# A 64-byte filler tile at the right end of SBUF, in a two-mixture kernel on one core

## The chip, the cores and the metric

The kernel runs on one core of one Trainium2 chip. The metric is the device time of one execution, in microseconds (us); less is better. Each core has a tensor engine (TensorE; PE in the profile, its weight loads PEld), a vector engine (DVE), a scalar engine (ACT), GpSimd (POOL) and a sync engine (SP) that issues the DMA transfers. All operands of these engines stand in SBUF (128 partitions) or, for results of TensorE, in PSUM.

## What is computed

A recurrent attention, a first mixture (three matrix products with a gating multiply) and a second mixture of 8 experts, whose weights are normalised by eight rounds over rows and columns. The second mixture takes most of the time:

```python
def _moe2_ref(x, w_gate, w1, w2):            # x: 3072 x 384
    logits = x @ w_gate
    P = np.exp(logits - logits.max())
    for _ in range(8):
        P /= P.sum(1, keepdims=True) + 1e-09
        P /= P.sum(0, keepdims=True) + 1e-09
        P *= N / E
    for e in range(E):                       # 8 experts
        h = np.maximum(x @ w1[e], 0.0)       # w1[e]: 384 x 1024
        ye = h @ w2[e]                       # w2[e]: 1024 x 384
        out += P[:, e:e + 1] * ye
```

## The kernel before

**The three parts.** Attention, the first mixture and the conversion of its float64 weights run first, interleaved, up to about 442 us. The second mixture follows as 64 phases (line 1141: `for n in range(N + 1)`); the first of them still runs beside the last products of the first mixture (`moe_x2`, its PSUM tile is `po`).

**A phase.** Phase n belongs to weight step k = n // 4 (one quarter of an expert) and to one batch, sb = n % 4. In it stand 15 products of a fast matrix-multiplication scheme (line 543, `ORDER`), each with 2 column halves j and 3 float32 pieces (high by high, high by low, low by high): 15 x 2 x 3 = 90 matmuls into PSUM tiles `zp` (`z_prod`, line 869). Their moving operand is a slice of `xc` with 256 columns, their stationary operand a slice of `w1c` with 128 columns. Between the products stand units of the output product of the phase before (`y_fill`, line 1039, called by `y_units`): 24 units with 3 matmuls each, 72 into PSUM tiles `yp`, with a moving operand `w2h` or `w2l` of 384 columns and a stationary operand `hh` or `hl`. So a phase of the middle holds 162 matmuls. Every one loads its own weights (LDWEIGHTS), in the order in which the program is written: the schedule is by hand (line 104) and no planner moves anything.

**Which buffer a phase uses.** `w1c` has three sets by i % 3 and `w2h`, `w2l` have four by i % 4, where i = 2k + j is the weight number (lines 640 and 659). Set 2 of `w1c` and sets 2 and 3 of `w2h`, `w2l` lie in the pool `m2` on the left side of SBUF; the other sets and all of `xc` lie in the pools `wp` and `m1` on the right side, which is filled from the upper end downwards. `hh` and `hl` are always in `m2`. So k % 3 decides where the weights of the `zp` matmuls stand (0: both halves on the right; 1: half j = 0 on the left; 2: half j = 1 on the left), and k % 2 decides where the moving operand of the `yp` matmuls stands (even: right, odd: left; the first phase of a k still uses those of the k before).

**The addresses.** A matmul operand begins at its tile's address plus a multiple of 512 bytes, so its remainder modulo 128 is that of the tile. In bytes within a partition, as the program places them:

```
tile                       pool, side     address before   mod 128   after    mod 128
xc0, xc1                   wp, right      149472, 161760     96      149408 ..  32
xc2, xc3                   m1, right       90080, 104416     96       90016 ..  32
w1c, sets 0 and 1          wp, right      145376 ...         96      145312 ..  32
w1c, set 2                 m2, left        71456 ...         32      the same   32
w2h, w2l, sets 0 and 1     m1, right      126944 ...         96      126880 ..  32
w2h, w2l, sets 2 and 3     m2, left        55072 ...         32      the same   32
hh, hl                     m2, left        22304 ...         32      the same   32
gh, gl, w34h, w34l (po)    moe, left       44896 ...         96      the same   96
```

Counted over the program before, 3960 of the 5760 `zp` matmuls have weights with remainder 96 and 1800 with 32, all with a moving operand at 96; of the 4608 `yp` matmuls, all with weights at 32, half have a moving operand at 96 and half at 32.

Of the kernel before, what the change touches and what calls it, by code (L numbers as in the profile page):

```python
# [11 lines left out]
F32 = mybir.dt.float32  # L12
# [49 lines left out]
def tile_rwkv_moe_sinkhorn_moe(  # L62
# [21 lines left out]
    P = 128  # L84
# [51 lines left out]
    for c in range(2):  # L136
        nc.scalar.activation(eye[64 * c:64 * c + 64, :], ident[64 * c:64 * c + 64, 64 * c:64 * c + 64], AF.Copy)
        nc.gpsimd.affine_select(out=mask[64 * c:64 * c + 64, :], in_=mask[64 * c:64 * c + 64, :],
                                compare_op=ALU.is_gt, fill=0.0, base=0, pattern=[[1, DP]],
                                channel_multiplier=-1)  # L140

    st_moe = ExitStack()
    moe = st_moe.enter_context(tc.tile_pool(name="moe", bufs=1))
# [1095 lines left out]
```

## Time and profile before

| | |
|---|---|
| three runs | 1945.58, 1946.57 and 1946.62 us, median 1946.57 |
| profiled execution, span from first to last instruction | 1946.4 us |
| PE busy | 1919.9 us, 99% of the span |
| DVE, ACT, POOL busy | 1381.8, 686.2, 647.2 us |
| DMA engines, mean busy share | 51.4% for the kernel's own transfers |
| granted TensorE clock | 1.00 (2.4 GHz) in every stretch |

The profile gives no total of its own for the profiled execution; its span is taken as its time. A row of the timeline shows when a run of like instructions starts and how many there are. Matmuls are pipelined: the duration that a row gives for one is longer than the distance from its start to the next start, and that distance is what a matmul costs where PE never idles. A row of the windows shows the busy time of each engine in a stretch, and the number of instructions with any part in it.

### The profile page before, as it was taken

What the parts mean: (1) busy time and instruction counts of PE and PEld (TensorE: products, weight loads), DVE (VectorE), ACT (ScalarE), POOL (GpSimd) and SP (SyncE); (2) the same over time, 40 slices, a digit from 0 to 9 for tenths busy, and PEclk for the clock granted to TensorE, in tenths of its full rate; (3) what the DMA queues carried; (4) which work ended last, traced back from release to release, by engine and by line L of the source; (5) the groups of instructions that cost most, each with busy time, mean ns of one, the idle gap of its engine ahead of it and who ended that gap; (6) DMA issues with size and microseconds to landing.
All of it is one profiled execution on the core that took longest, in us unless ns stands there. A gap on an engine that the chain in (4) does not pass through costs nothing.

```text
span 1946.4 us, 38115 instructions
## 1 busy us (share of the span) xinstructions
PE 1919.9 (99%) x15499; PEld 1872.1 (96%) x15499; DVE 1381.8 (71%) x2409; ACT 686.2 (35%) x1322; POOL 647.2 (33%) x867
## 2 busy tenths in 40 slices
PE   6999999999999999999999999999999999999999
PEld 3799999999999999999999999999999999999999
DVE  7865777765887876666767676666676767667666
ACT  6733333344333333233333233333333333333322
POOL 6856666635332312222222222221313231312200
PEclk9999999999999999999999999999999999999999
DMA  9632444347655555454545555555454555555453
GB/s 371 228 95 81 138 132 137 104 151 247 224 177 202 184 190 187 174 213 172 202 177 193 186 193 181 187 185 195 172 202 176 199 188 186 188 179 189 167 202 118
DMA packets 90494, 353.76 MB, mean 182 GB/s; under 512 B 10384, under 2 KB 34256, under 8 KB 64592
## 3 DMA queue, kind: packets, MB, share of 16 engines
q1 hardware_dynamic: 90320, 351.34, 51.4%
q8 instruction: 122, 2.00, 0.4%
q14 instruction: 52, 0.43, 0.1%
HBM read 329.67 MB, written 20.45 MB: 180 GB/s over the span
## 4 chain that ended last, share of the span: by engine, by line
PE 96%; DVE 2%; DMA 1%; ACT 1%; issue 0%; SPq 0%; DVEq 0%; ACTq 0%
PE yp L114 41%; PE zp L114 35%; PE po L114 5%; PE pa L114 5%; PE pb L114 4%; PE w34ps L114 2%; PE yt L114 1%; PE sc L114 1%; PE trn L114 1%; PE up L114 1%; DMA raw<-in_moe_w_out_dram 0%; PE pl L114 0%; DMA raw<-in_moe_w_dram 0%; DVE cvp L229 0%; DMA xraw<-xraw 0%
## 5 line engine op out<-in xcount | busy, mean ns | idle before, releaser
L114 PE MATMUL zp<-xc,w1c 128*128 128x256 f32 x5760 | 815.4, 281 | 1.0 <-DVE ct L894 0.5
L114 PEld LDWEIGHTS zp<-xc,w1c 128*128 128x128 f32 x5760 | 783.6, 189 | 3.8 <-DVE ct L897 1.4
L114 PE MATMUL yp<-w2h,hh 128*128 128x384 f32 x1536 | 516.9, 337 | 0.0
L114 PE MATMUL yp<-w2h,hl 128*128 128x384 f32 x1536 | 516.3, 336 | 0.5 <-DVE hl L891 0.5
L114 PE MATMUL yp<-w2l,hh 128*128 128x384 f32 x1536 | 513.9, 335 | 0.0
L886 ACT ACTIVATE hh<-ct 128x512 fp32r<-128x512 f32 x384 | 237.1, 632 | 538.1 <-DVE ct L894 269.8
L894 DVE TENSOR_TENSOR ct<-ct,zp 128x512 f32<-128x512 f32 x576 | 381.0, 683 | 53.2 <-PE zp L114 47.5
L616 POOL TENSOR_TENSOR w1c<-w1s,w1c 128x512 fp32r<-128x512 f32 (+1 forms) x120 | 127.7, 1064 | 796.4 <-PE yp L114 487.9
L901 ACT ACTIVATE ct<-zp 128x512 f32<-128x512 f32 x256 | 153.3, 599 | 455.9 <-PE zp L114 455.9
L114 PEld LDWEIGHTS yp<-w2h,hh 128*128 128x128 f32 x1536 | 290.9, 189 | 0.2 <-issue 0.2
L114 PEld LDWEIGHTS yp<-w2h,hl 128*128 128x128 f32 x1536 | 288.1, 188 | 1.0 <-DVE hl L891 0.9
L114 PEld LDWEIGHTS yp<-w2l,hh 128*128 128x128 f32 x1536 | 288.3, 188 | 0.0
L1066 DVE SCALAR_TENSOR_TENSOR acc<-yp,Pm,acc 128x384 f32<-128x384 f32 x336 | 205.5, 612 | 109.4 <-PE yp L114 109.2
L891 DVE SCALAR_TENSOR_TENSOR hl<-ct,hh 128x512 fp32r<-128x512 f32 x384 | 273.8, 726 | 0.0
L897 DVE TENSOR_TENSOR ct<-ct,zp 128x512 f32<-128x512 f32 x128 | 88.0, 688 | 168.4 <-PE zp L114 168.4
L897 DVE TENSOR_TENSOR ct<-zp,ct 128x512 f32<-128x512 f32 x128 | 88.3, 690 | 78.2 <-PE zp L114 69.6
L616 POOL TENSOR_TENSOR w1c<-w1raw,w1c 128x128 fp32r<-128x128 f32 (+1 forms) x90 | 55.0, 612 | 205.6 <-ACT w1c L612 205.6
L608 POOL TENSOR_TENSOR w1s<-w1raw 128x128 f32<-128x128 f32 x240 | 121.0, 525 | 0.2
L483 POOL TENSOR_TENSOR gl<-gs,gh 128x384 fp32r<-128x384 f32 x64 | 74.2, 1160 | 109.3 <-ACT gh L479 106.6
L114 PE MATMUL pa<-xhl,w1h 128*128 128x384 f32 x384 | 101.7, 345 | 1.2 <-ACT w34s L255 1.2
L114 PE MATMUL pb<-xhl,w2h 128*128 128x384 f32 x384 | 98.1, 336 | 0.4 <-DVE cv L230 0.4
L474 DVE TENSOR_TENSOR gs<-pb,asb 128x384 f32<-128x384 f32 x64 | 35.4, 553 | 71.5 <-PE pb L114 49.3
(130 smaller groups left out, 1906.2 us busy)
## 6 DMA issues: line engine op xcount, KB each, us to landing
xc<-xd SPq DMA_DIRECT2D x192, 1024.0 KB, 4.8
xc<-xd SPq DMA_DIRECT2D x64, 768.0 KB, 4.3
xd<-x2s SPq DMA_DIRECT2D x53, 256.0 KB, 2.8
w1raw<-in_e_w_dram SPq DMA_DIRECT2D x32, 384.0 KB, 3.1
w2raw<-in_e_w_dram SPq DMA_DIRECT2D x32, 384.0 KB, 3.1
raw<-in_moe_w_dram SPq DMA_DIRECT2D x8, 1024.0 KB, 8.9
nat_w<-in_w_dram SPq DMA_DIRECT2D x24, 264.5 KB, 3.3
nat_k<-in_kt_dram SPq DMA_DIRECT2D x24, 256.0 KB, 4.0
```

Of the source, the lines that this page charges most:

```text
L114: nc.tensor.matmul(o, lhsT, rhs, start=start, stop=stop, **kw)
L474: nc.vector.tensor_tensor(t, m_t.pop(("pb", blk, f)), m_t.pop(("asb", blk, f)), op=ALU.mult)
L483: nc.gpsimd.tensor_tensor(gl[:, f, :], m_t.pop(("gs", blk, f)), gh[:, f, :].bitcast(F32), op=ALU.subtract)
L608: eng.tensor_tensor(tmp_[:, many.index(r), :], at_(a), at_(b), op=ALU.add if sg == 1 else ALU.subtract)
L616: eng.tensor_tensor(lo[:, d0:d1, :], sv, hi[:, d0:d1, :].bitcast(F32), op=ALU.subtract)
L886: nc.scalar.activation(hh, src, AF.Relu)
L891: nc.vector.scalar_tensor_tensor(hl, src, 0.0, hh.bitcast(F32), op0=ALU.max, op1=ALU.subtract)
L894: nc.vector.tensor_tensor(o, a, b_, op=ALU.add)
L897: nc.vector.tensor_tensor(o, a, b_, op=ALU.subtract)
L901: nc.scalar.activation(t, src, AF.Copy)
L1066: nc.vector.scalar_tensor_tensor(dst, yp, so["Pm"][:, tt, e:e + 1], dst, op0=ALU.mult, op1=ALU.add)
```

## The change

The change adds a pool on the right side of SBUF, opened ahead of all other pools of that side, with one tile of 16 float32 (64 bytes in each partition). Nothing reads or writes the tile. Every later tile on the right side lies 64 bytes lower. No instruction is added, removed or moved, and every wait stays: the instructions of the two programs agree one by one but for addresses, on every engine.

```diff
@@ -138,6 +138,9 @@
         nc.gpsimd.affine_select(out=mask[64 * c:64 * c + 64, :], in_=mask[64 * c:64 * c + 64, :],
                                 compare_op=ALU.is_gt, fill=0.0, base=0, pattern=[[1, DP]],
                                 channel_multiplier=-1)
+
+    edge = ctx.enter_context(tc.tile_pool(name="edge", bufs=1, side="right"))
+    edge.tile([P, 16], F32, name="edge")
 
     st_moe = ExitStack()
     moe = st_moe.enter_context(tc.tile_pool(name="moe", bufs=1))
```

## Rows read from the trace of the kernel before

**Rows 1.** The page: span, busy time by engine, chain that ended last.
```profile
span 1946.4 us, 38115 instructions
...
PE 1919.9 (99%) x15499; PEld 1872.1 (96%) x15499; DVE 1381.8 (71%) x2409; ACT 686.2 (35%) x1322; POOL 647.2 (33%) x867
...
PE yp L114 41%; PE zp L114 35%; PE po L114 5%; PE pa L114 5%; PE pb L114 4%; PE w34ps L114 2%; PE yt L114 1%; PE sc L114 1%; PE trn L114 1%; PE up L114 1%; DMA raw<-in_moe_w_out_dram 0%; PE pl L114 0%; DMA raw<-in_moe_w_dram 0%; DVE cvp L229 0%; DMA xraw<-xraw 0%
```

**Rows 2.** Windows, four stretches; the second holds phases 4 to 62.
```profile
core 0: us, PE busy (x) PEld busy (x) DVE busy (x) ACT busy (x) POOL busy (x), PEclk, DMA share, GB/s
442.02:540.07 98.05, 96.47 (x677) 94.53 (x677) 70.11 (x132) 37.06 (x78) 45.99 (x64) 1.00 0.69 243
540.07:1907.07 1367.00, 1367.00 (x9569) 1365.27 (x9569) 969.80 (x1567) 445.10 (x821) 328.81 (x537) 1.00 0.53 188
0.00:442.02 442.02, 420.64 (x5021) 376.76 (x5022) 320.54 (x677) 197.38 (x415) 272.38 (x266) 1.00 0.47 158
1907.07:1946.40 39.33, 35.83 (x235) 35.49 (x234) 21.38 (x35) 6.64 (x11) 0.00 (x0) 1.00 0.25 86
```

**Rows 3.** Waits of PE: who, for whom, total us, times, longest.
```profile
PE sc L114 <- POOL Rt L312: 14.0, 1, 14.0
...
PE yp L114 <- DVE hl L891: 0.5, 1, 0.5
PE zp L114 <- DVE ct L894: 0.5, 1, 0.5
PE zp L114 <- DVE ct L897: 0.5, 2, 0.2
```

**Rows 4.** Windows on PE, one whole phase each: 39, 27, 31, 43, 47, 35.
```profile
core 0: us, PE busy (x), PEclk, DMA share, GB/s
1351.40:1374.59 23.19, 23.19 (x163) 1.00 0.48 170
1073.87:1097.18 23.32, 23.32 (x163) 1.00 0.48 170
1166.48:1189.50 23.02, 23.02 (x163) 1.00 0.50 172
1444.14:1467.41 23.27, 23.27 (x163) 1.00 0.49 170
1536.63:1559.73 23.09, 23.09 (x163) 1.00 0.47 171
1258.69:1281.73 23.04, 23.04 (x163) 1.00 0.48 172
```

**Rows 5.** Timeline of PE at the start of phase 39.
```profile
1351.40 0.87 PE L114 MATMUL zp<-xc,w1c 128*128 128x256 f32 x6
1352.11 0.34 PE L114 MATMUL yp<-w2h,hh 128*128 128x384 f32 x1
```

**Rows 6.** Timeline of PE at the start of phase 40.
```profile
1374.59 0.86 PE L114 MATMUL zp<-xc,w1c 128*128 128x256 f32 x6
1375.28 0.34 PE L114 MATMUL yp<-w2h,hh 128*128 128x384 f32 x1
```

**Rows 7.** Timeline of PE in phase 0, where `zp` alternates with `po`.
```profile
446.26 0.88 PE L114 MATMUL zp<-xc,w1c 128*128 128x256 f32 x6
...
456.79 0.88 PE L114 MATMUL zp<-xc,w1c 128*128 128x256 f32 x6
457.51 0.34 PE L114 MATMUL po<-gh,w34l 128*128 128x384 f32 x1
...
458.03 0.33 PE L114 MATMUL po<-gh,w34l 128*128 128x384 f32 x1
...
458.90 0.88 PE L114 MATMUL zp<-xc,w1c 128*128 128x256 f32 x6
459.61 0.34 PE L114 MATMUL po<-gl,w34h 128*128 128x384 f32 x1
```

## The prediction

> **What bounds the kernel now.** I read the page first: PE is busy for 1919.9 of 1946.4 us, and the chain that ended last is the row of PE's own matmuls, `yp` 41% and `zp` 35% [rows 1]. Then the windows by part: from 540.07 to 1907.07 us, phases 4 to 62, PE is busy all of 1367.00 us, while DVE is busy for 969.80, ACT for 445.10 and POOL for 328.81 of it [rows 2]. Then PE's waits: all that `zp` and `yp` wait for other engines are 1.5 us, and the one long wait, 14.0 us, belongs to attention [rows 3]. The granted clock is 1.00, 2.4 GHz, in each stretch [rows 2]. So in 59 of 64 phases the time is the number of matmuls times the distance from start to start, and nothing else. The change alters no instruction and no wait; it can act only by making that distance longer or shorter, or not at all.
>
> Next I cut the span at the starts of phases. A phase holds the same 162 matmuls every time, and yet not all take as long [rows 4]. Phases differ in where their operands stand, which k % 3 and k % 2 decide. In the order of the rows, with the remainders modulo 128 of the weights of `zp` for j = 0 and j = 1, and of the moving operand of `yp` (the moving operand of `zp` is at 96 and the weights of `yp` at 32 throughout):
>
> - phase 39: 96, 96; 32: 23.19 us
> - phase 27: 96, 96; 96: 23.32 us
> - phase 31: 32, 96; 32: 23.02 us
> - phase 43: 32, 96; 96: 23.27 us
> - phase 47: 96, 32; 32: 23.09 us
> - phase 35: 96, 32; 96: 23.04 us
>
> The spread is 0.30 us, 1.3% of a phase, with no idle time in any. So placement does count, and the mean over phases 4 to 62 is 1367.00 / 59 = 23.169 us [rows 2].
>
> **What the change does, part by part.**
>
> *The tile itself.* It is 64 bytes that nothing touches, with no instruction and no wait. Its cost is nothing, and no cover is needed.
>
> *The six kinds of phase become one.* Right-hand tiles go from remainder 96 to 32, left-hand tiles stay at 32. So in every phase the weights of `zp` are 32, 32, the moving operand of `zp` goes from 96 to 32, that of `yp` is 32, the weights of `yp` stay at 32. This seventh kind occurs nowhere before. What to take for it?
>
> The clue is which pairs differ. In phase 39 each matmul's two operands have the same remainder, and in phase 40, of the kind of phase 31, the first three `zp` of a run have different ones. At their starts, six `zp` take 1352.11 - 1351.40 = 0.71 us in the first [rows 5] and 1375.28 - 1374.59 = 0.69 us in the second [rows 6]. Read so, what helps is a difference between moving operand and weights, not the remainder 32 as such, and the change takes every difference away.
>
> One stretch of the trace has no difference at all: phase 0, where `zp` at 96, 96 alternates with `po`, also 384 columns wide, both of whose operands stand at 96. That is the new arrangement shifted by 64 bytes. From 446.26 to 458.90 us there are six periods of 6 `zp` and 8 `po`, so one takes 12.64 / 6 = 2.107 us; in it the six `zp` take 457.51 - 456.79 = 0.72 and 459.61 - 458.90 = 0.71 us, and the eight `po` 458.90 - 457.51 = 1.39 us, 0.174 us each; the first three of them, after the `zp`, take 0.52 us, so no gain hides at the seam [rows 7]. A full phase has 15 sixes of `zp` and 72 wide matmuls: nine such periods are 18.96 us and hold all 72 and nine sixes; six more sixes at 0.718 us are 4.31 us. Together 23.27 us. That is more than the phase's mean of 23.169 us, and I take it.
>
> *The sum.* Phases 4 to 62: 59 x 23.27 = 1372.9 us against 1367.00, so +5.9 us. Phase 63, of the kind of phase 39, goes from 23.19 to 23.27, +0.1 us. Phases 1 to 3, of the kind of phase 27, go from 23.32 to 23.27, which is 0.15 us back in all; they also hold stalls, which the change does not touch. Phase 0 turns the other way round: its `zp` move to 32 while `po` stays at 96, which makes it like phase 39, 0.1 us less at most. I write +6 us. The span of 1946.4 us lies 0.2 us under the median of the runs, so on the median this makes 1946.57 + 6.0 = **1952.6 us**, 0.3% slower.
>
> *The bounds of the unknown.* The two kinds whose `zp` have equal remainders throughout are nearest: 23.19 us gives 59 x 23.19 = 1368.2, +1.2 us, so 1947.8; 23.32 us gives 1375.9, +8.9 us, so 1955.5. I keep these as ends of the main case and take 23.27, because phase 0 alone has both kinds of matmul and all their operands at one remainder. Farther out, on the fast side, stands 23.02 us.
>
> *Ahead of phase 0.* The raw and converted weights of the first mixture (pool `tmp`) and the tiles `x2s` move as well. PE is busy 420.64 of 442.02 us there [rows 2], but of its matmuls only the 64 of `w34ps` and the 72 of `pl` have an operand on the right. `w34ps` is 2% of the chain and `pl` 0% [rows 1], so some 39 us; if these changed by the whole spread of 1.3%, it would be 0.5 us in either direction. I take nothing and keep 0.5 us for the range.
>
> *Other engines and DMA.* DVE, ACT and POOL read and write the moved tiles too. DVE, the busiest, has 1367.00 - 969.80 = 397 us to spare in 59 phases [rows 2], so even an operation a tenth longer would hide. The DMA engines are busy for about half of that stretch. Cost nothing.
>
> **A rule that speaks against it.** The rows say that two operands at different remainders go together better than two at the same: 0.69 against 0.71 us for six [rows 5, 6]. The Trainium skill, page "TensorE: Matmul & The Clock Gate", section "Step-by-step: what each phase is for", says that TensorE reads the moving operand and the weights through two independent ports of SBUF, and that loading the next weights takes nothing from the running matmul. By that rule no pair of placements could matter and the sum would be 0, 1946.6 us. The spread of the phases is not explained by it, so I keep it as a rival with a small chance.
>
> **The rivals.**
>
> 1. *Faster: the weights' own remainder counts.* Of the two kinds with `yp` at 32 that differ only in j = 0, weights at 32 are faster by 23.19 - 23.02 = 0.17 us [rows 4]. If 32 is simply the good remainder for weights, both halves at 32 give 23.19 - 0.34 = 22.85 us, 59 x 22.85 = 1348.2, 18.8 us less: 1927.8 us. For it: of the four kinds with a half at 32, three are the fastest of all six. Against it: with `yp` at 96 the same step is worth only 23.32 - 23.27 = 0.05 us, and with j = 1 and `yp` at 32 only 0.10 us; a property of the weights alone would be worth the same each time. A milder form, all phases at the best kind's 23.02, is 59 x 23.02 = 1358.2, 8.8 us less: 1937.8 us. It decides from a phase under 23.10 us on. Chance 0.16 for both.
> 2. *The change does nothing.* What differs between phases is not the remainder but the distance between tiles or the side of SBUF on which they stand, which the change leaves as it was but for 64 bytes. For it: set 2 of `w1c` differs from the others in both. Against it: the kinds with the same `w1c` differ by the place of `w2h` alone, and back and forth (faster by 0.05 us at 96 for k % 3 = 2, slower by 0.25 us for k % 3 = 1), which a distance would not give easily. Time 1946.6 us. Chance 0.14, the rule on two ports with it.
> 3. *Worse than forecast.* All phases as slow as phase 27: 1955.5 us, with 0.5 us from the first part 1956. This is the upper end of the main case.
>
> **How the numbers follow.** The main case, equal remainders cost what phases 39, 27 and 0 show, has 0.70 and lies between 1947.8 and 1955.5 us. A measurement of this kernel can tell about 0.2%, 3.9 us, from no change, so slower begins at 1950.5. Of the 0.70 I put 0.62 above that, because phase 0 is the nearest stretch, and 0.08 below. Slower is then 0.62, the same 0.14 + 0.08 = 0.22, faster 0.16. The range reaches from 1946.0, which takes in "nothing", to 1956.5, and leaves out the faster rival and a little above: about 2 in 10.
>
> **What would show it.** In the profile after, all phases from 4 on should take one and the same time, near 23.27 us, whatever k is, with six `zp` after a wide matmul in 0.72 us and a wide matmul in 0.174 us; PE still busy without a gap, DVE not longer by more than a tenth. If the phases still differ in the old pattern, remainders were not the cause. If they are all alike and near 22.85 or 23.02 us, the remainder of the weights counted. If the span grew outside phases 4 to 63, the sum was made in the wrong place.

## The result and the profile after

The change made the kernel slower: 1959.54 us, median of 5 runs (1958.45 to 1960.23), against 1946.05 us before (1945.58 to 1946.62, 5 runs). The ratio is 1.0067, 95% interval 1.0055 to 1.0079. The forecast was 1952.6 us with a range up to 1956.5: the direction came out, but the time grew by 13.5 us where 6.0 were forecast.

The page of the kernel after, first its span and busy times:

```profile
span 1958.5 us, 38115 instructions
...
PE 1932.5 (99%) x15499; PEld 1885.2 (96%) x15499; DVE 1384.4 (71%) x2409; ACT 686.8 (35%) x1322; POOL 644.6 (33%) x867
```

The span of the profiled execution grew by 12.1 us and PE's busy time by 12.6 [rows 1]; DVE, ACT and POOL moved by less than 3 us each, with the same instructions. Next the stretches that answer to [rows 2]: phases 4 to 62 in one view, and what lies ahead of them and behind them in another.

```profile
540.41:1919.10 1378.69, 1378.69 (x9569) 1377.59 (x9569) 971.80 (x1567) 445.74 (x821) 326.69 (x537) 1.00 0.53 186
```

```profile
0.00:442.30 442.30, 421.19 (x5025) 377.18 (x5026) 321.37 (x678) 197.69 (x415) 272.19 (x266) 1.00 0.47 158
442.30:540.41 98.11, 96.72 (x674) 94.84 (x673) 69.82 (x132) 36.72 (x77) 45.71 (x64) 1.00 0.70 243
1919.10:1958.50 39.40, 35.92 (x235) 35.57 (x234) 21.41 (x35) 6.63 (x11) 0.00 (x0) 1.00 0.25 86
```

Phases 4 to 62 take 1378.69 us where they took 1367.00: 11.69 of the 12.1 us are there. PE is busy in all of it, at a granted clock of 1.00 (2.4 GHz) as before, and DVE still has 407 us to spare. The other three stretches together grew by 0.41 us. So no wait was added; the same 9569 rows of matmuls stand farther apart. PE's waits say the same: the waits of `zp` and `yp` are as small as in [rows 3].

```profile
PE zp L114 <- DVE ct L897: 0.5, 1, 0.5
...
PE yp L114 <- DVE hl L894: 0.4, 1, 0.4
```

Last the single phases, in the order of [rows 4]: 39, 27, 31, 43, 47, 35. Columns: stretch, its length, PE busy (rows), granted clock, DMA share, GB/s.

```profile
1358.89:1382.16 23.27, 23.27 (x163) 1.00 0.47 170
1078.53:1101.90 23.37, 23.37 (x163) 1.00 0.47 170
1172.26:1195.77 23.51, 23.51 (x163) 1.00 0.50 169
1452.43:1475.81 23.38, 23.38 (x163) 1.00 0.47 170
1545.54:1568.72 23.18, 23.18 (x163) 1.00 0.48 170
1265.63:1288.97 23.33, 23.33 (x163) 1.00 0.48 170
```

They are not all alike. Phase 39 is at 23.27 us, to the hundredth what was forecast for every phase; phase 31, one of the fastest before at 23.02, is now the slowest of the six at 23.51, and phase 47 stays at 23.18. The mean over the 59 phases is 1378.69 / 59 = 23.368 us, three phases with ten further small matmuls among them (`pcs`, of the normalisation, in phases 4 to 6).

What phase 39 has and the others lack is that the operands of a matmul are on one side of SBUF: `xc` and `w1c` both right, `w2h` and `hh` both left. In the table of addresses, right and left now agree modulo 128; modulo 256 they don't. Left tiles of the second mixture stand at 32 modulo 256 (55072, 71456, 22304); right tiles stood at 224 before (145376, 149472) and stand at 160 after. The **distance**, right minus left, modulo 256, was 192 and is 128.

### The profile page after: what moved, and what is told of

The parts are those of the page before. It is cut to its first block, busy times and chain, and to the rows that moved or that the text cites. A ratio compares the mean times of both kernels' runs of the same rounds, so it can differ in the third digit from the quotient of the medians.

```text
span 1958.5 us, 38115 instructions
## 1 busy us (share of the span) xinstructions
PE 1932.5 (99%) x15499; PEld 1885.2 (96%) x15499; DVE 1384.4 (71%) x2409; ACT 686.8 (35%) x1322; POOL 644.6 (33%) x867
## 4 chain that ended last, share of the span: by engine, by line
PE 94%; DMA 2%; DVE 2%; ACT 1%; issue 0%; SPq 0%; DVEq 0%; ACTq 0%
PE yp L114 41%; PE zp L114 35%; PE po L114 5%; PE pa L114 5%; PE pb L114 4%; DMA raw<-in_moe_w_dram 2%; PE yt L114 1%; PE w34ps L114 1%; PE sc L114 1%; PE trn L114 1%; DMA nat_kn<-in_kn_dram 1%; PE up L114 0%; PE pl L114 0%; DMA xraw<-xraw 0%; DVE Gt L286 0%
```

## The experiments

Each kernel was timed together with the kernel before; ratios are to that kernel, with 95% intervals. The expectations name their theories as they were held when each set was planned; the sets are the three parts below. In all of these kernels the instructions are those of the kernel before, in the same order; only addresses differ. "The six phases" are 39, 27, 31, 43, 47, 35, in this order.

### First set: remainder modulo 128, distance modulo 256, or alignment

**Filler of 192 bytes** (distance 0 modulo 256, remainder 32 modulo 128 as in the change).

```diff
-    edge.tile([P, 16], F32, name="edge")
+    edge.tile([P, 48], F32, name="edge")
```

> The filler has 192 bytes in place of 64. Right-hand operands then have remainder 32 modulo 128 as in the change, but they also agree with the left-hand ones modulo 256 and 512 (288 on both sides), where in the change they differ by 128 bytes. Theory A (only the remainder modulo 128 counts): the same as the change, 1959.5 us, with phases between 23.18 and 23.51 us. Theory B (placement counts modulo 256 or more): one kind of phase for every k, near the 23.27 us that the change shows where all operands of both products share one side; 59 x 23.27 = 1372.9 us in phases 4 to 62, so about 1953 us. Theory C (the side of SBUF itself counts): the pattern of the change, 1959.5 us.

1950.18 us, ratio 1.0017 [1.0008, 1.0027]. Phases 39 and 31, and phases 4 to 62:

```profile
1352.06:1375.26 23.20, 23.20 (x163) 1.00 0.49 170
...
1166.46:1189.66 23.20, 23.20 (x163) 1.00 0.49 171
...
538.64:1908.86 1370.22, 1370.22 (x9569) 1.00 0.53 187
```

Here is the one kind of phase that the forecast had looked for: all six last 23.20 us. This kernel and the change have the same remainders modulo 128 in every tile, and differ by 8.5 us in these phases. What counts goes beyond 128.

The same kernel settles whether other engines or the DMA, whose tiles move too, have a part in it. Phases 41 and 42, with the columns of [rows 2]:

```profile
1398.46:1421.66 23.20, 23.20 (x163) 23.18 (x163) 15.71 (x26) 8.30 (x18) 11.39 (x19) 1.00 0.53 188
1421.66:1444.86 23.20, 23.20 (x163) 23.18 (x163) 17.24 (x28) 7.60 (x14) 0.00 (x0) 1.00 0.58 205
```

GpSimd is busy for 11.39 us of the one and for nothing of the other, DVE for 15.71 and 17.24 us, the DMA engines for 53% and 58%, and both last 23.20 us. In this layout nothing but PE's own matmuls shows in a phase's time.

**Filler of 128 bytes** (remainders modulo 128 as in the kernel before, distance 64 modulo 256):

```diff
-    edge.tile([P, 16], F32, name="edge")
+    edge.tile([P, 32], F32, name="edge")
```

> The filler has 128 bytes. The right-hand operands are back at remainder 96 modulo 128, as before the change, but the distance from right to left is 64 bytes modulo 256 where before it is 192. Theory A: the same as before, 1946.1 us, and the six kinds of phase at 23.02 to 23.32 us. Theory B: not the times of before phase by phase; total unknown, between 1940 and 1962 us. Theory C: 1946 to 1959 us.

1951.93 us, ratio 1.0027 [1.0017, 1.0038]. The six phases: 23.42, 23.34, 23.13, 23.02, 23.01, 23.32. Of these, phases 39, 31, 47 and 35, and phases 4 to 62:

```profile
1352.16:1375.58 23.42, 23.42 (x163) 1.00 0.49 169
...
1165.89:1189.02 23.13, 23.13 (x163) 1.00 0.49 171
...
1537.13:1560.14 23.01, 23.01 (x163) 1.00 0.47 172
1258.65:1281.97 23.32, 23.32 (x163) 1.00 0.48 170
538.16:1909.13 1370.97, 1370.97 (x9569) 1.00 0.52 187
```

By remainders modulo 128 this had to be the pattern of [rows 4], 23.19 for phase 39 and 23.04 for phase 35. Phase 39 is 0.23 us longer and phase 35 0.28 us. The theory of remainders modulo 128 falls.

**64 bytes in the left pool instead**, as the first tile of `m2`, and no filler at the right end (right tiles stay where they were before; left tiles of `m2` go to 96 modulo 256; distance 128, as in the change):

```diff
+        m2.tile([P, 16], F32, name="pad")
```

> No filler on the right; instead 64 bytes at the start of the left pool of the second mixture. All operands then begin at 96 modulo 128, and the distance between the sides is 128 bytes modulo 256, as in the change. If only the placement of operands relative to each other counts: the phases of the change, 1959.5 us. If 32 is the better remainder by itself, as the faster rival had it: slower than the change, above 1962 us. If 96 is the better one: clearly faster than 1959 us.

1959.06 us, ratio 1.0063 [1.0048, 1.0078]. Phases 39, 31, 47 and 4 to 62:

```profile
1357.36:1380.63 23.27, 23.27 (x163) 1.00 0.47 170
...
1170.73:1194.23 23.51, 23.51 (x163) 1.00 0.48 169
...
1544.02:1567.20 23.18, 23.18 (x163) 1.00 0.48 170
...
538.87:1917.58 1378.71, 1378.71 (x9569) 1.00 0.52 186
```

The change's own phase times, each within 0.01 us, and 1378.71 against 1378.69 in all, though every operand stands at another remainder than in the change. So the remainder of a tile by itself means nothing; where two tiles stand to each other does.

**32 bytes on the right and 32 on the left** (distance 128 again, but every operand of the second mixture begins at a multiple of 64):

```diff
-    edge.tile([P, 16], F32, name="edge")
+    edge.tile([P, 8], F32, name="edge")
...
+        m2.tile([P, 8], F32, name="pad")
```

> 32 bytes on the right and 32 bytes in the left pool, so that every operand of the second mixture begins at a multiple of 64 bytes (64 modulo 128), with the same distances between the sides as in the change. If the start within 64 bytes does not count: the phases of the change, 1959.5 us. If each operand is read in blocks of 64 bytes, one block less for each of 10368 matmuls: six zp at 6 x (0.1183 - 0.0067) and yp at 0.174 - 0.0067, so 69 us less, about 1890 us; twice that, about 1821 us, if blocks of 128 bytes count.

1958.94 us, ratio 1.0062 [1.0047, 1.0077]. Phase 39, phase 31, and phases 4 to 62:

```profile
1358.52:1381.79 23.27, 23.27 (x163) 1.00 0.49 170
...
1171.88:1195.39 23.51, 23.51 (x163) 1.00 0.48 169
...
540.02:1918.72 1378.70, 1378.70 (x9569) 1.00 0.52 186
```

Again the change's times. Beginning at a multiple of 64 bytes brings nothing here.

### Second set: the period, and placing operands on purpose

**Filler of 256 bytes**:

```diff
-    edge.tile([P, 16], F32, name="edge")
+    edge.tile([P, 64], F32, name="edge")
```

> The filler has 256 bytes. Distances between the sides agree with those of the kernel before modulo 256, not modulo 512. If placement counts modulo 256: the phases of before one by one, 23.19, 23.32, 23.02, 23.27, 23.09 and 23.04 us, and 1946.7 us. If it counts modulo 512 or more: other phases, 1940 to 1962 us. If the side of SBUF or the distance itself counts: other phases too.

1946.75 us, ratio 0.9999 [0.9990, 1.0008]. Phases 39, 31 and 4 to 62:

```profile
1350.07:1373.26 23.19, 23.19 (x163) 1.00 0.50 170
...
1165.20:1188.21 23.01, 23.01 (x163) 1.00 0.47 172
...
538.93:1905.68 1366.74, 1366.74 (x9569) 1.00 0.53 188
```

The six phases are 23.19, 23.31, 23.01, 23.27, 23.10, 23.03: those of [rows 4] within 0.01 us. The period of the distance between the sides is 256 bytes or a divisor of it, and 128 and 64 are excluded by the kernels above.

The next three, and the first three of the third set, are edits of the kernel before, without the filler at the right end. A pad of 192 bytes in `m2` brings left and right to the same place modulo 256; chosen tiles are then shifted, in `wp` and `m2` by allocating 256 bytes more and using a view, in `m1` by a pad behind them or ahead of the pool:

```diff
+        m2.tile([P, 48], F32, name="pad")
...
+    def shifted(pool, shape, off, tag, name):
+        n_ = shape[0] * shape[1] * shape[2]
+        t = pool.tile([P, n_ + 64], F32R, tag=tag, name=name)
+        return t[:, off // 4:off // 4 + n_].rearrange("p (a b c) -> p a b c", a=shape[0], b=shape[1])
```

**All moving operands 192 bytes behind all weights** (`xc` and `w2h`, `w2l` shifted by 192):

```diff
+            t = shifted(pools["w"], (2, len(XP_[g][4]), T), 192, f"xc{g}", f"xc{g}")
...
+            hi = shifted(pool, (1, 2, DM), 192, f"w2h{k}", f"w2h{k}")[:, 0]
+            lo = shifted(pool, (1, 2, DM), 192, f"w2l{k}", f"w2l{k}")[:, 0]
...
+    mpad.tile([P, 16], F32, name="mpad")
```

(`mpad`, 64 bytes ahead of the pool `m1`, puts all of that pool 64 bytes lower, which is 192 modulo 256.)

> All stationary operands of the second mixture begin at 224 modulo 256 and all moving ones at 160, so that each matmul's moving operand stands 192 bytes after its weights modulo 256, whatever the product. By theory B there is one kind of phase. If what counts is a matmul's moving operand against its own weights: zp as in the halves with different remainders before, 113 to 116 ns each instead of 118, so a phase of 22.8 to 23.0 us, and 1924 to 1937 us. If what counts is a matmul's moving operand against the weights that load beside it for the next one, the same, since both are one distance here. If only the seams between zp and yp count: near 23.20 us, 1950 us.

1928.91 us, ratio 0.9909 [0.9894, 0.9924]. Phase 39 and phases 4 to 62; all six phases are 22.86:

```profile
1339.73:1362.59 22.86, 22.86 (x163) 1.00 0.47 173
...
538.15:1888.37 1350.22, 1350.22 (x9569) 1.00 0.54 190
```

**Only `xc` 192 bytes behind**, all else alike:

```diff
+        if g < 2:
+            t = shifted(pools["w"], (2, len(XP_[g][4]), T), 192, f"xc{g}", f"xc{g}")
...
+        if i == 0:
+            pool.tile([P, 16], F32, name="wpad")
```

(`wpad` lies in `m1` between `xc3` and `w2h`; the pool ends where it did, so `xc2` and `xc3` come to lie 64 bytes lower.)

> As with 160 for the moving and 224 for the stationary operands, but for zp alone: xc begins at 160 modulo 256, everything else, the moving operands of yp too, at 224. If each matmul's moving operand against its own weights counts: zp as fast as with all moving operands at 160, yp as with all operands alike (174.2 ns): phase 22.8 to 23.0 us if yp does not profit, so within 0.1 us of that run. If seams count, another time, between 22.9 and 23.4 us.

1925.15 us, ratio 0.9891 [0.9876, 0.9905]: faster than the kernel before and the change, and the fastest of all that ran. Phase 39 and phases 4 to 62; all six are 22.80:

```profile
1338.23:1361.03 22.80, 22.80 (x163) 1.00 0.48 173
...
538.57:1885.43 1346.86, 1346.86 (x9569) 1.00 0.54 190
```

The timeline of PE shows which matmuls gained. A row: start, duration of the run, what, how many. First after, at the start of phase 39, then this kernel, inside its phase 39:

```profile
1358.89 0.88 PE L114 MATMUL zp<-xc,w1c 128*128 128x256 f32 x6
1359.61 0.34 PE L114 MATMUL yp<-w2h,hh 128*128 128x384 f32 x1
```

```profile
1345.17 0.84 PE L114 MATMUL zp<-xc,w1c 128*128 128x256 f32 x6
1345.85 0.34 PE L114 MATMUL yp<-w2h,hh 128*128 128x384 f32 x1
...
1347.41 1.52 PE L114 MATMUL zp<-xc,w1c 128*128 128x256 f32 x12
1348.77 0.34 PE L114 MATMUL yp<-w2h,hh 128*128 128x384 f32 x1
```

From start to start, six `zp` take 0.72 us after the change and 0.68 here; the twelve in a row shown take 1.36 us, 113 ns each. Summed over phase 39 in this way, from starts to the nanosecond, the 90 `zp` take 10.75 us after the change, 10.65 before, 10.66 with the filler of 192, 10.22 here. The `yp` take the rest, 12.52 to 12.58 us in all four. So the gain is in `zp`.

**Only `w2h`, `w2l` shifted, by 64 bytes** (the moving operands of `yp`):

```diff
+            hi = shifted(pool, (1, 2, DM), 64, f"w2h{k}", f"w2h{k}")[:, 0]
+            lo = shifted(pool, (1, 2, DM), 64, f"w2l{k}", f"w2l{k}")[:, 0]
...
+            pool.tile([P, 16], F32, name="wpad")
...
+    mpad.tile([P, 48], F32, name="mpad")
```

> The moving operands of yp alone stand 64 bytes after their weights modulo 256, everything else is alike. zp should then stay at the 118.4 ns that it has with all operands alike, except at seams; yp: the rows of before show 174.1 ns with its operands alike and 174.3 with 64 bytes between, so no gain: phase 23.15 to 23.30 us, 1946 to 1956 us.

1952.86 us, ratio 1.0029 [1.0017, 1.0040]; all six phases 23.23:

```profile
1354.48:1377.71 23.23, 23.23 (x163) 1.00 0.49 170
...
540.03:1912.08 1372.04, 1372.04 (x9569) 1.00 0.53 187
```

Little beside 23.20 with nothing shifted, and in the wrong direction. (The rows of before that the expectation compares with have the operands of `yp` 192 bytes apart, not 64.)

### Third set: which pairs matter

**Only `xc` shifted, by 128**; against the kernel with `xc` at 192:

```diff
-            t = shifted(pools["w"], (2, len(XP_[g][4]), T), 192, f"xc{g}", f"xc{g}")
+            t = shifted(pools["w"], (2, len(XP_[g][4]), T), 128, f"xc{g}", f"xc{g}")
...
-            pool.tile([P, 16], F32, name="wpad")
+            pool.tile([P, 32], F32, name="wpad")
```

> xc 128 bytes after its weights modulo 256 in place of 192, all else alike as there. If any difference between a matmul's own two operands serves: zp at 113.5 ns as with 192, phase 22.80 us, 1925 us. If 128 bytes is the bad distance that made the change slower than forecast: zp at 120 ns or more, phase 23.3 to 23.6 us, 1954 to 1972 us.

1958.67 us, ratio 1.0064 [1.0049, 1.0079]; all six phases 23.35:

```profile
1356.85:1380.20 23.35, 23.35 (x163) 1.00 0.48 169
...
538.13:1917.42 1379.30, 1379.30 (x9569) 1.00 0.53 186
```

One distance of 128 bytes, between `xc` and everything else, costs as much in phases 4 to 62 as the whole change (1379.30 against 1378.69 us), with no side of SBUF in it. Against the same kernel at 192 it is 32.4 us.

**`xc`, `w2h`, `w2l`, `hh` and `hl` all at 192, `w1c` at 0.** Within each matmul the distances are those of the fast kernel (`zp` 192, `yp` 0); only between a `zp` and the `yp` beside it are they others. To the edits of the kernel with all moving operands at 192 come two pads, ahead of `hh`, `hl` and behind them:

```diff
+        m2.tile([P, 48], F32, name="hpad")
...
+            pools["m2"].tile([P, 16], F32, name="hpad2")
```

> xc 192 bytes after w1c, as in the fastest run so far; the operands of yp agree with each other as there, but both stand 192 bytes after w1c. So each matmul's own two operands have the same distances as in that run, and only the distances across the seams between zp and yp differ. If a matmul's own pair is all that counts: 22.80 us a phase and 1925 us. If the seams count: another time; the rows of before allow 0.1 to 0.2 us a phase, 6 to 12 us, up or down.

1948.86 us, ratio 1.0013 [1.0004, 1.0023]; all six phases 23.20:

```profile
1350.56:1373.76 23.20, 23.20 (x163) 1.00 0.48 170
...
537.30:1907.36 1370.06, 1370.06 (x9569) 1.00 0.53 187
```

All of the gain is gone: the 90 `zp` of phase 39 take 10.61 us. A matmul's own pair does not decide by itself.

**`xc` at 192 and `hh`, `hl` at 64** (the own pairs of both matmuls at 192, `xc` to `hh` at 128). To the edits of the kernel with only `xc` at 192 come:

```diff
+        m2.tile([P, 16], F32, name="hpad")
...
+            pools["m2"].tile([P, 48], F32, name="hpad2")
```

> xc 192 bytes after w1c as in the fastest run so far, and the weights of yp moved by 64 bytes, so that the moving operands of yp stand 192 bytes after their own weights too. With 192 bytes in both, yp took 173.4 ns where all moving operands stood at 160 modulo 256, against 174.8 with yp alike; zp lost part of its gain there. If the own pair counts: zp 113.5 and yp 173.4 ns, 72 x 1.4 ns less than 22.80 us a phase, so 22.70 us and about 1919 us. If the seams cost what zp lost there, 22.86 us and 1929 us.

1946.96 us, ratio 1.0004 [0.9994, 1.0013]; all six phases 23.17:

```profile
1350.94:1374.12 23.17, 23.17 (x163) 1.00 0.48 170
...
539.01:1906.74 1367.73, 1367.73 (x9569) 1.00 0.53 188
```

The gain is missing here too: the 90 `zp` take 10.65 us. Of the four kernels with `xc` 192 bytes behind `w1c`, the two in which it also stands 192 behind `hh` and `hl`, the weights of the `yp` beside it, are fast (22.80, 22.86), the other two are not.

That is no account of single matmuls, though. In phase 39 of these four kernels every `zp` reads the very same addresses of `xc` and `w1c`; of the matmuls' operands only those of `yp` have moved. From that phase of the kernel with all moving operands at 192, a run of six and a run of twelve:

```profile
1339.73 0.85 PE L114 MATMUL zp<-xc,w1c 128*128 128x256 f32 x6
1340.41 0.33 PE L114 MATMUL yp<-w2h,hh 128*128 128x384 f32 x1
...
1348.96 1.58 PE L114 MATMUL zp<-xc,w1c 128*128 128x256 f32 x12
1350.37 0.34 PE L114 MATMUL yp<-w2h,hh 128*128 128x384 f32 x1
```

The six take 0.68 us, 113 ns each, and the twelve 1.41 us, 118 ns each, at the same distances. In the two kernels without the gain the twelves take 1.41 or 1.42 us too; with only `xc` shifted they take 1.39 and 1.36. Ten of a run of twelve have only `zp` ahead of them and behind them. So the place of the operands of `yp` reaches into `zp` that do not stand beside a `yp`, and neither a `zp`'s own pair nor the matmul next to it says what it costs. How that comes about is not shown.

**Filler of 32 bytes** (distance 160, between before and after):

```diff
-    edge.tile([P, 16], F32, name="edge")
+    edge.tile([P, 8], F32, name="edge")
```

> The change with 32 bytes of filler in place of 64: distance between the sides 160 modulo 256, half way between before (192) and the change (128). If placement counts in blocks of 64 bytes from a fixed grid: some operands fall on the block of before and some on that of the change, a time between 1946.7 and 1959.5 us or outside. If it changes smoothly with the distance: about 1953 us.

1956.47 us, ratio 1.0052 [1.0037, 1.0067]. Phases 39, 43, 35 and 4 to 62:

```profile
1356.52:1379.86 23.35, 23.35 (x163) 1.00 0.48 169
...
1449.52:1472.70 23.18, 23.18 (x163) 1.00 0.47 172
...
1263.06:1286.49 23.43, 23.43 (x163) 1.00 0.49 169
539.67:1915.58 1375.91, 1375.91 (x9569) 1.00 0.53 186
```

In all between before and after, but phase 39 (23.35) and phase 35 (23.43) are longer than in either, and phase 43 (23.18) is shorter. Half a step of 64 does count; whether the effect runs smoothly between steps this doesn't settle.

## Why the prediction came out as it did

**What bounds the kernel: right.** PE never idles in phases 4 to 62, and 11.69 of 12.1 us appeared there, by the distance between starts alone.

**The tile, other engines, DMA, the part ahead of phase 0: right.** The part ahead of phase 0 grew by 0.28 us, inside the 0.5 us that was kept for it, and DVE's busy time in phases 4 to 62 by 2.00 us of 970. Phase 0 with phases 1 to 3 grew by 0.06 us where some tenths less were forecast.

**"The six kinds of phase become one": wrong, and the step that failed.** It took operands with the same remainder modulo 128 for alike. The runs showed that the place that counts is modulo 256, and relative: moving the left side by 64 bytes gives the change's times phase by phase, moving the right side by 256 gives those of before, by 128 neither. The change brought right and left to 128 bytes apart, not together, so six kinds stayed. The kernel in which they do become one is the one with a filler of 192, at 23.20 us a phase. There, taking every difference away costs 3.2 us in phases 4 to 62 (1370.22 against 1367.00); the other 8.5 us of the change come of the distance of 128, which the prediction did not see. That the direction came out is in good part luck.

**The price of 23.27 us from phase 0: right for one kind of phase in six, mis-sized for the rest.** Phase 0 before has `xc` and `w1c` at 224 and `po`'s operands at 96 modulo 256: equal within each matmul, 128 apart between neighbours. That is what phase 39 has after the change, and it came out at 23.27. The other kinds have the 128 bytes also inside their matmuls; in the sum, 59 x 23.27 = 1372.9 us became 1378.69, 5.8 us more. Some 1.4 us of this is a term that the sum leaves out, the `pcs` matmuls of phases 4 to 6, which the 1367.00 us of before contain (with the filler of 192, 59 x 23.20 = 1368.8 us against 1370.22 measured). The upper bound failed with it: 23.32 us was the worst kind of before, and four of the six kinds lie above it. Rival 3, all phases like phase 27, was the nearest, and still 3.5 us short.

**The clue behind it was half right.** A difference between the operands of `zp` did help before: that of `w1c` set 2, at 32, to `xc`, at 224, is 192 modulo 256, which in every `zp`, with all operands of `yp` where the weights of `zp` stand, makes 22.80 us. But it is not difference as such that helps: 128 in its place makes 23.35 and none 23.20.

**Rival 1, the weights' remainder 32: wrong.** All operands at 96 modulo 128 gave the same times as all at 32, as long as the distance was kept. Its time of 1927.8 us was near what the same tiles give when they are placed at 192 (1925.15), for another reason.

**Rival 2, nothing changes: wrong in its time, right in naming the distance between tiles.** The Trainium skill, page "TensorE: Matmul & The Clock Gate", section "Step-by-step: what each phase is for", gives TensorE two independent read ports, so that loading weights takes no read bandwidth from the running matmul. What the prediction drew from it, that no pair of placements could matter, does not hold in these runs: the same instructions take 1346.86 to 1379.30 us in phases 4 to 62, by the place of `xc` alone. Whether it is at the ports or elsewhere that the operands meet, no run shows.

**What stays open.** What in the chip makes the distance count was not shown, nor how the place of the operands of `yp` changes the time of `zp` that read the same addresses. Phase 43 of [rows 4], with half its `zp` at 192 and no gain to speak of, is not explained. `xc` at 64, and mixed placements better than 22.80 us, were not tried.

## What to carry to other kernels

Where the profile shows PE busy without a gap and stretches of the same matmuls that differ by a per cent, the places of their operands are worth looking at: compare them modulo 256 bytes and against each other, over all the matmuls that alternate there, not each by its own remainder. A padded tile is a cheap trial, here worth 1.1% in one place and minus 0.7% in another, but a trial it is, since the good distance (192 for `xc` alone) was found and not derived. Before a stretch is taken as a price for another, ask in how many relations they agree: the one used here fitted one kind of phase to the hundredth and missed the rest.

## What the hardware showed unexpectedly

- Identical instruction streams, on a PE that does not idle in 59 of 64 phases, at a granted clock of 1.00, differ by 1.7% in time (1925.15 to 1958.67 us) by shifting one operand by 64 bytes.
- Beginning at a multiple of 64 bytes does nothing (1958.94 against 1959.54 us); the distance modulo 256 does.
- `zp` that read the same addresses take 113 or 118 ns each: twelve of them 1.36 us with only `xc` shifted and 1.41 us where operands of the `yp` between the runs are moved too; in the latter kernel six others still take 113 ns each.
- Phase times repeat closely: three different layouts with distance 128 between the sides gave 1378.69, 1378.71 and 1378.70 us for phases 4 to 62.
- A `zp` of 256 columns is not at a floor in the kernel before: 118 ns there (10.65 us for 90), 114 at 192 bytes (10.22 us for 90).
